# Two pairs of heads per run of scores, the first token's rows once for all batches, and another order of VectorE's steps, in a sink-window attention with Fourier mixing and a feed-forward block

## The chip, the core and the metric

The kernel runs on one core of a Trainium2 chip. The core has a matrix engine (TensorE; PE in the profile, with its weight loads as PEld), VectorE (DVE), ScalarE (ACT), GpSimd (POOL) and SyncE (SP), which issues most of the DMAs. Each engine works through its own list of instructions in order and waits on semaphores for the others. Sums of matmuls land in PSUM, which has eight banks; ACT and DVE copy them out. The metric is the device time of one execution in microseconds (us), the median of several runs. The profile is one execution; its span runs from its first to its last instruction.

## What is computed

Attention over 4 batches, 8 heads, 768 tokens of 64 values, in which each token sees the first four tokens (the sink) and the 127 before it and itself. Its output, 4 x 768 x 512, goes through a Fourier transform over tokens and channels, whose real part is added to it, and then through a feed-forward block.

```python
scores = scale * np.matmul(q, k.transpose(0, 1, 3, 2))
keep = is_sink | in_window
scores = np.where(keep, scores, -1000000000.0)
a = np.exp(scores - max); a = a / (sum(a) + 1e-09)
x = np.matmul(a, v)                       # then heads side by side: (4, 768, 512)
u = x + real(fft(fft(x, axis=1), axis=2))
un = (u - mean(u)) / sqrt(var(u) + 1e-06)
out = u + np.maximum(un @ w_ch1, 0.0) @ w_ch2
```

All of it is in 32-bit precision. Products that need more than one pass of the fast matmul type split a value into a high and a low part (names with `hi` and `lo`).

## The kernel before

**Steps.** The attention goes over 24 blocks g of 128 tokens (6 per batch), and in a block over 4 pairs of heads hp. One step s = 4 g + hp handles one pair; k = s % 4 is the place in the block. `window_attention` is a software pipeline: at step s, `scores` runs for step s itself, and the other stages run for earlier steps, by `STEP_LAG`: `merge` and `soft1` one step later, `expo` two, `trans_p` three (for two pairs at once, at even k), `copy_p` four, `newer_p` and `older_p` five, `av` seven (also at even k). Stages that run once a block have their distance in `BLOCK_AT`: `trans_sink` 7 (so at k = 3), `copy_sink` 8, `inverse` 7, `turn_x` 12, `store_x` 13, and `sink_lo`, once a batch, 2.

**What a step does.** `scores` (L721; L719 in the first block of a batch) multiplies 64-row halves of PE by the keys, for two heads side by side, into one of two PSUM buffers "s". On DVE, `merge` (L727) selects between two key blocks and `soft1` (L739) scales, masks and finds the maximum, which frees the buffer. ACT does the exponential (`expo`, L745). PE turns the result (`trans_p`, L770, bank "pt"), ACT copies it out (`copy_p`, L777), GpSimd cuts it into two triangles (L786, L794), and PE multiplies by the values (`av`, L808, output xt, on 64-column halves). `trans_sink` (L826) turns the sink's part, also in the bank "pt", and `copy_sink` (L831) copies it out. `turn_x` (L820, L822) and `store_x` (L836) bring the block into `u`.

**The order on each engine** up to step 97 (`CUT`) is written out by hand: `SCHEDULE[s >= 36][engine][k]` lists the stages, and between them the names in `EVENTS`: "A", "V", "G", "T" and the digits 0 to 3, places where work registered by `at(step, place, fn)` is put. "T" is work on PE, "V" and the digits are on DVE. "S" is work of SP's queue and runs ahead of the step's scores. From step 97 on a planner chooses the order, and it may set that work between the steps written by hand.

**The transform.** When the fourth block of a batch is stored (steps 25, 49, 73, 97), `fourier` registers its parts at distances from there. Folds (`fold_n`, `fold_m`, L348 to L358, on DVE and GpSimd) at 3, 4, 7, 8, 11 and 12, their split (L361 on ACT, `fold_lo`, L364, on DVE) three to four steps later; PE's first stage (`stage1`, L393) from 15 on; then its second (L420, L441). Each stage's result is copied out of the one bank "fft" (at k = 2 another bank, "x", is used in some steps), by `z_hi`, `z_lo`, `combine` and their like. For batches 0 to 2 many parts are cut in two, one in each of two steps.

**The first token.** Token 0 is no row of the six blocks of 128 that come out of attention; its output is made on 32 partitions (batch x head) at steps 10 to 20 and stored to DRAM (`x0_dram`). Each batch's `fourier` loads it broadcast to 33 partitions (`load_row`, L343), and at distance 5 copies its row into `u` (`put_row`, L379), at 8 folds it (`mid_sum`, L368), and at 10 splits it into rows 0 and 32 of `sph` (`mid_hi`, L371, and `mid_row`, L376), which PE's first stage reads.

**After attention** come the weight conversion (L600 to L602 on DVE), the first group of the feed-forward block (L638, L1139) and the five others (L638, L1313).

Of the kernel before, what the change touches and what calls it, by code (L numbers as in the profile page):

```python
# [11 lines left out]
F32 = mybir.dt.float32  # L12
# [7 lines left out]
P = 128  # L20
# [44 lines left out]
F_N, F_M, F_S, ROW = (3, 3), (4, 5), (6, 7), (5, 8, 10)  # L65
# [4 lines left out]

STEP_LAG = {"merge": 1, "soft1": 1, "expo": 2, "sink_p": 2, "trans_p": 3, "copy_p": 4, "newer_p": 5, "older_p": 5, "av": 7}
# [21 lines left out]
            ["merge", "inverse", "store_x", "sink_lo", "V", "soft1", 3, 0, 1, 2],  # L93
            [3, "merge", 1, "V", "soft1", "inverse", "store_x", 0, "sink_lo", 2],
            ["sink_lo", 0, "merge", 3, 1, "V", 2, "soft1", "store_x", "inverse"],
            ["merge", "inverse", 0, "soft1", "V", 3, "store_x", "sink_lo", 2, 1],
# [22 lines left out]
            ["merge", "inverse", "store_x", "sink_lo", "soft1", 3, 1, 0, "V", 2],  # L119
            [2, "merge", 0, "sink_lo", 3, 1, "V", "soft1", "inverse", "store_x"],  # L120
            ["sink_lo", 0, "merge", "soft1", 3, "V", 2, 1, "store_x", "inverse"],
            ["merge", 1, "inverse", 3, 2, "soft1", "store_x", "V", 0, "sink_lo"],
# [89 lines left out]
def kernel(  # L212
# [28 lines left out]
    x0_dram = dpool.tile([B * H, D], F32, name="x0d")  # L241

# [24 lines left out]
    def run(general):  # L267
        tag = "g" if general else ""
        with ExitStack() as p1:
# [58 lines left out]

            def fourier(b, at, ready):
# [11 lines left out]
                def load_row():  # L341
                    t_["x0"] = fw.tile([NR, DM], F32, tag="xr", name=f"xr_{b}")
                    nc.sync.dma_start(t_["x0"], x0_dram[H * b:H * b + H].rearrange("(o h) d -> o (h d)", o=1).broadcast_to([NR, DM]))  # L343
# [22 lines left out]
                def mid_sum():  # L366
                    r = t_["x0"]
                    V.tensor_tensor(r[:, 1:256], r[:, 1:256], r[:, 511:256:-1], op=ALU.add)  # L368

                def mid_hi():  # L370
                    (A.copy if b == B - 1 else V.tensor_copy)(sph[:NR, :257], t_["x0"][:, :257])  # L371

                def mid_row():
                    t = t_["x0"]
                    lo = sph[NR - 1:NR, :257]
                    V.tensor_tensor(lo, t[NR - 1:NR, :257], f32(lo), op=ALU.subtract)  # L376

                def put_row():
                    V.tensor_copy(u[NHALF][0:1], t_["x0"][0:1])  # L379
# [83 lines left out]
                at(1, "S", load_row)  # L463
# [10 lines left out]
                at(ready[0] + ROW[0], "V", put_row)  # L474
                at(ready[0] + ROW[1], "V", mid_sum)
                at(ready[0] + ROW[2], "A" if b == B - 1 else "V", mid_hi)
                at(ready[0] + ROW[2], "V", mid_row)
# [176 lines left out]
            def window_attention(fourier, load_constants):  # L654
                with ExitStack() as pa:
# [168 lines left out]
                    def trans_sink(g):  # L824
                        ps = ps_t.tile([P, P], F32R, tag="pt", name=f"pk_{g}")
                        T.transpose(ps, st.pop(("sk", g)).rearrange("p g h s -> p (g h s)"), ident_r)  # L826
                        st["pk", g] = ps
# [16 lines left out]
                    with ExitStack() as man:  # L844
# [117 lines left out]
                        for i in range(NS):  # L962
                            at(17 + i, "V", lambda i=i: first_row(i))

# [6 lines left out]
                        s = 0  # L971
                        extra.append(lambda name: ps_t.tile([P, 512], F32, tag="x", name=name)
                                     if s % NP in X_AT and not X_NOT[0] <= s <= X_NOT[1] and s < len(steps) - 2 else None)
                        while s < last:
# [19 lines left out]
                            if k == 3 and wraps:  # L994
                                load_qk(g + 2)
                            if s == 0:
# [3 lines left out]
                            for e in "AVGT":  # L1000
                                for op in SCHEDULE[s >= PHASE][e][k]:
                                    if op in EVENTS:
# [16 lines left out]
            def general_attention(fourier):  # L1019
                for b in range(B):  # L1020
# [74 lines left out]
                    ev = []  # L1095
# [506 lines left out]
```

## Time and profile before

| | |
|---|---|
| median of 3 runs | 768.49 us (767.43 to 771.24) |
| the profiled execution's own time | 768.74 us |
| its span | 767.0 us |
| mean granted clock of PE | 0.995 |
| score pairs in the trace | 96 steps: 320 matmuls L721, 64 matmuls L719 |
| softmax passes (L739) | 192, mean 285 ns |
| queue of SP | 94352 packets, 124.26 MB |

The views that follow in the prediction are read so. The page's first part gives each engine's busy time, its share of the span and its instructions. A view of stages gives the same for each stretch of time, with the granted clock as a share of full speed. A row of the view of waits says which instruction group waited for which, how long in all, how often, and the longest. The chain goes back from the last instruction to what released it at each step: a start, a length, and what ran. In a timeline, a start and a duration of each instruction; on DVE, the next starts before the last one's end is written, so the distance between starts is what one costs.

### The profile page before, as it was taken

How to read it: one execution, taken by the hardware profiler on the slowest of the kernel's cores; microseconds unless marked ns; L12 is line 12 of the kernel's file. 1: busy time of each engine (PE TensorE's matmuls, PEld its weight loads, DVE VectorE, ACT ScalarE, POOL GpSimd, SP SyncE). 2: the span in 40 equal slices, each digit the busy share in tenths (PEclk: the TensorE clock that was granted, in tenths of full speed). 3: DMA queues.
4: the chain of work that ended last, by engine and by line, in shares of the span. 5: the costliest groups of instructions: out<-in, count | busy, mean ns of one | idle time of the engine just before them, and what ended most of it. 6: DMA issues, size and time to landing. Idle time of an engine off the chain costs nothing.

```text
span 767.0 us, 14157 instructions
## 1 busy us (share of the span) xinstructions
PE 742.3 (97%) x4903; PEld 626.7 (82%) x4903; DVE 600.6 (78%) x1641; ACT 345.9 (45%) x896; POOL 181.6 (24%) x286
## 2 busy tenths in 40 slices
PE   7999998998999999999999999999999999999996
PEld 5666775766788778788989899899899998998995
DVE  6878588799799989969877978778895888764435
ACT  4877666666643223444545333333333333333330
POOL 2557267467574445400000000000000000000001
PEclk9999999999999999999999999999999999999998
DMA  9845514532313446323546757755577557556661
GB/s 294 277 112 165 144 56 151 160 104 94 111 56 138 138 165 219 110 110 141 190 151 247 227 160 231 230 171 191 170 226 235 173 172 243 160 176 188 208 193 60
DMA packets 95008, 129.40 MB, mean 169 GB/s; under 512 B 5932, under 2 KB 60844, under 8 KB 94544
## 3 DMA queue, kind: packets, MB, share of 16 engines
q1 hardware_dynamic: 94352, 124.26, 51.1%
q0 software_dynamic: 288, 3.76, 1.3%
q8 instruction: 41, 0.67, 0.4%
q10 hardware_dynamic: 288, 0.39, 0.1%
q14 instruction: 39, 0.32, 0.1%
HBM read 104.26 MB, written 24.13 MB: 167 GB/s over the span
## 4 chain that ended last, share of the span: by engine, by line
PE 78%; DVE 16%; issue 2%; ACT 1%; POOL 1%; DMA 1%; SPq 0%; DVEq 0%; ACTq 0%; POOLq 0%
PE h L638 31%; PE p L1313 25%; PE xt L808 5%; PE s L721 5%; PE o L1139 3%; PE pt L770 2%; PE za L393 2%; PE zb L393 1%; DVE f L348 1%; PE x L820 1%; DVE sm L739 1%; DVE gl L364 1%; PE zr L393 1%; DVE w2r L602 1%; DMA vt<-in_v_sink_dram 1%
## 5 line engine op out<-in xcount | busy, mean ns | idle before, releaser
L1313 PE MATMUL p<-w_ring,h_sums 128*128 128x256 f32 x936 | 131.3, 283 | 0.1
L1313 PEld LDWEIGHTS p<-w_ring,h_sums 128*128 128x128 f32 x936 | 122.9, 191 | 3.6 <-DVE u L1143 0.3
L1261 ACT CAST h_sums<-sums 128x256 fp32r<-128x256 f32 (+2 forms) x158 | 89.7, 568 | 70.5 <-PE p L1313 28.6
L1262 DVE TENSOR_TENSOR h_sums<-sums,h_sums 128x256 fp32r<-128x256 f32 (+2 forms) x158 | 98.3, 622 | 17.5 <-ACT h_sums L1261 16.5
L1313 PE MATMUL p<-w2t,h_sums 128*128 128x256 f32 x702 | 110.3, 283 | 0.0
L1335 POOL TENSOR_TENSOR u<-u,u 128x512 f32<-128x512 f32 x3 | 3.8, 1293 | 422.9 <-DVE u L1335 422.9
L1313 PEld LDWEIGHTS p<-w2t,h_sums 128*128 128x128 f32 x702 | 97.9, 191 | 3.1
L638 PE MATMUL h<-un_slots,w 128*128 128x512 f32 x396 | 96.5, 392 | 0.0
L638 PE MATMUL h<-un_last,w 128*128 128x512 f32 x396 | 96.4, 392 | 0.0
L638 PEld LDWEIGHTS h<-un_slots,w 128*128 128x128 f32 x396 | 72.7, 188 | 14.0
L638 PEld LDWEIGHTS h<-un_last,w 128*128 128x128 f32 x396 | 72.3, 188 | 14.4 <-DVE un_slots L553 0.7
L745 ACT ACTIVATE sm<-sm,mx 128x132 f32<-128x132 f32 x192 | 75.8, 399 | 14.4 <-DVE mx L739 14.4
L1475 ACT ACTIVATE sums<-h 128x512 f32<-128x512 f32 x40 | 23.9, 597 | 96.8 <-PE h L638 96.8
L721 PE MATMUL s<-ring,q 64*128 64x260 f32 x320 | 55.6, 430 | 7.2 <-DVE mx L739 7.2
L1163 DVE STREAM_TRANSPOSE unf<-un 32x128 f32<-32x128 f32 x192 | 58.1, 302 | 2.8
L1272 DVE TENSOR_TENSOR sums<-sums 128x256 f32<-128x256 f32 x39 | 16.4, 422 | 47.6 <-ACT sums L1475 47.3
L1443 ACT ACTIVATE sums<-h 128x512 f32<-128x512 f32 x40 | 23.9, 599 | 64.8 <-PE h L638 64.8
L739 DVE CUSTOM_DVE_ANT_0 sm<-s,mask 128x132 f32<-128x132 f32 x192 | 47.5, 285 | 4.5 <-PE s L719 2.4
L727 DVE COPY_PREDICATED s<-older,s 128x256 f32<-128x256 uint8 x80 | 33.8, 422 | 16.9 <-PE s L721 16.6
L721 PEld LDWEIGHTS s<-ring,q 64*128 64x128 f32 x320 | 25.0, 186 | 21.3 <-issue 10.0
L808 PE MATMUL xt<-ptl,ldv 128*64 128x128 f32 x384 | 39.8, 288 | 0.0
L745 ACT ACTIVATION_READ_ACCUMULATOR sm<-sm,mx 128x1 f32 x192 | 36.7, 191 | 0.0
(239 smaller groups left out, 1378.1 us busy)
## 6 DMA issues: line engine op xcount, KB each, us to landing
w_ring<-w2s SPq DMA_DIRECT2D x62, 512.0 KB, 4.3
w2t<-w2s SPq DMA_DIRECT2D x93, 256.0 KB, 3.2
raw<-in_moe_w_ch_dram SPq DMA_DIRECT2D x32, 512.0 KB, 3.3
w2s<-w_ring SPq DMA_DIRECT2D x16, 512.0 KB, 3.0
ldv<-in_v_dram SPq DMA_DIRECT2D x28, 256.0 KB, 2.8
ring<-in_qk_dram SPq DMA_DIRECT2D x24, 264.0 KB, 4.3
w2s<-w2t SPq DMA_DIRECT2D x24, 256.0 KB, 3.1
out_dram<-u SPq DMA_DIRECT2D x22, 256.0 KB, 4.6
```

The lines of the kernel that those rows point to most:

```text
L393: T.matmul(ps[:, :NK], a, c, start=i == 0, stop=i == len(mm) - 1)
L638: T.matmul(ps[:, :tb], a[:, cs], x[:, :, cc, :], start=n == 0, stop=n == 3 * NCC - 1)
L721: T.matmul(ps[:, j, :P + W], st["q", g][rows, hp, :], keys(g, 2 * hp + j), start=True, stop=True)
L727: V.copy_predicated(ps[:, :, P + NS:P + W], older[qi > 2], ps[:, :, 0:P])
L739: V.tensor_tensor_reduce(sm[:, h % 4], ps[:, j, P:P + W], mask[min(qi, 3)], -SCALE, 3.0e38, ALU.add, ALU.min, accum_out=mx[:, 0, h:h + 1])
L745: A.activation(sm[:, h % 4], sm[:, h % 4], AF.Exp, bias=mx[:, 0, h:h + 1], scale=-1.0, accum_out=mx[:, 1, h:h + 1])
L808: T.matmul(ps[D * j:D * j + D, p, :], st["v", kb(g) - i][:, h, :], a[:, h % 4, :], start=i == 0, stop=i == n - 1)
L1163: V.transpose(unf[32 * q:32 * q + 32, :, r], un[r].rearrange("p (c q j) -> p c q j", c=NCC, q=4)[:, :, q])
L1261: A.copy(hc_hi[:, left(a, n)], src)
L1262: V.tensor_tensor(hc_lo[:, left(a, n)], src, f32(hc_hi[:, left(a, n)]), op=ALU.subtract)
L1313: T.matmul(acc[i][:, 2 * P * tp:2 * P * tp + 2 * P], x, w, start=q == 0 and tp == 0 and n == 0, stop=q == end and n == 2, skip_group_check ...
L1443: A.activation(r4[:, 0].rearrange("p t w -> p (t w)"), ps, AF.Relu)
```

## The change

It has four parts.

1. Between steps 9 and 96, at odd k, PE's list no longer runs "T" and `trans_sink` at their place: they are put into `hold` and run in the next step, behind its scores. So scores of an odd step and of the even step after it stand next to each other. `bank` decides by the step to which the work belongs (`at_s`).
2. `trans_sink` uses the bank "fft" in place of "pt" as long as its step is under 36.
3. DVE's lists become the same in both phases: `merge` and `soft1` first in every step, then what belongs to that k, then the digit 1, then "V". (The digits 0, 2 and 3, which fall out, hold no work; stages appear only at the k at which they can run.)
4. The first token's rows are made once: `middle_rows` loads them for all four batches on four partitions at step 24, folds them at 26 (DVE), splits them at 27 (ACT) and 28 (DVE), and stores both parts to DRAM (`xm_dram`) at 29. Each batch then loads rows 0 and 32 of `sph` by DMA at distance 9, and `put_row` is a DMA at distance 5. `mid_sum`, `mid_hi` and `mid_row` are gone.

```diff
-F_N, F_M, F_S, ROW = (3, 3), (4, 5), (6, 7), (5, 8, 10)
+F_N, F_M, F_S, ROW = (3, 3), (4, 5), (6, 7), (9, 5)
+ROW_AT = 24, 26, 27, 28, 29
+HOLD = 9, 97
...
         "V": [
-            ["merge", "inverse", "store_x", "sink_lo", "V", "soft1", 3, 0, 1, 2],
-            [3, "merge", 1, "V", "soft1", "inverse", "store_x", 0, "sink_lo", 2],
-            ["sink_lo", 0, "merge", 3, 1, "V", 2, "soft1", "store_x", "inverse"],
-            ["merge", "inverse", 0, "soft1", "V", 3, "store_x", "sink_lo", 2, 1],
+["merge", "soft1", 1, "V"],
+            ["merge", "soft1", 1, "V", "store_x"],
+            ["merge", "soft1", "sink_lo", 1, "V"],
+            ["merge", "soft1", "inverse", 1, "V"],
         ],
...
-            ["merge", "inverse", "store_x", "sink_lo", "soft1", 3, 1, 0, "V", 2],
-            [2, "merge", 0, "sink_lo", 3, 1, "V", "soft1", "inverse", "store_x"],
-            ["sink_lo", 0, "merge", "soft1", 3, "V", 2, 1, "store_x", "inverse"],
-            ["merge", 1, "inverse", 3, 2, "soft1", "store_x", "V", 0, "sink_lo"],
+["merge", "soft1", 1, "V"],
+            ["merge", "soft1", 1, "V", "store_x"],
+            ["merge", "soft1", "sink_lo", 1, "V"],
+            ["merge", "soft1", "inverse", 1, "V"],
...
+            def middle_rows(b, n, at):
+                x = fw.tile([B, DM], F32, tag="xr", name=f"xr_{b}")
+                xm = fw.tile([B, 2, DM // 2 + 1], F32R, tag="xm", name=f"xm_{b}")
+                def load():
+                    nc.sync.dma_start(x[:n], x0_dram[H * b:H * (b + n)].rearrange("(o h) d -> o (h d)", o=n))
+                def fold():
+                    V.tensor_tensor(x[:n, 1:256], x[:n, 1:256], x[:n, 511:256:-1], op=ALU.add)
+                def hi():
+                    A.copy(xm[:n, 0], x[:n, :257])
+                def lo():
+                    V.tensor_tensor(xm[:n, 1], x[:n, :257], f32(xm[:n, 0]), op=ALU.subtract)
+                def store():
+                    nc.sync.dma_start(xm_dram[b:b + n], f32(xm[:n]))
+                for s, e, fn in zip(ROW_AT, "SVAVS", (load, fold, hi, lo, store)):
+                    at(s, e, fn)
...
                 def load_row():
-                    t_["x0"] = fw.tile([NR, DM], F32, tag="xr", name=f"xr_{b}")
-                    nc.sync.dma_start(t_["x0"], x0_dram[H * b:H * b + H].rearrange("(o h) d -> o (h d)", o=1).broadcast_to([NR, DM]))
+                    nc.sync.dma_start(f32(sph[:NR:NR - 1, :257]), xm_dram[b])
...
                 def put_row():
-                    V.tensor_copy(u[NHALF][0:1], t_["x0"][0:1])
+                    nc.sync.dma_start(u[NHALF][0:1], x0_dram[H * b:H * b + H].rearrange("(o h) d -> o (h d)", o=1))
...
-                at(1, "S", load_row)
+                at(ROW[0], "S", load_row)
...
-                at(ready[0] + ROW[0], "V", put_row)
-                at(ready[0] + ROW[1], "V", mid_sum)
-                at(ready[0] + ROW[2], "A" if b == B - 1 else "V", mid_hi)
-                at(ready[0] + ROW[2], "V", mid_row)
+                at(ready[0] + ROW[1], "S", put_row)
...
                     def trans_sink(g):
-                        ps = ps_t.tile([P, P], F32R, tag="pt", name=f"pk_{g}")
+                        pool, tag = (ps_fft, "fft") if NP * g + BLOCK_AT["trans_sink"] < PHASE else (ps_t, "pt")
+                        ps = pool.tile([P, P], F32R, tag=tag, name=f"pk_{g}")
...
+                        middle_rows(0, B, at)
...
+                        def run_held(step):
+                            nonlocal at_s
+                            at_s = step
+                            run_ev(step, "T")
...
                             lag(scores, s, 0)
                             if k == 3 and wraps:
                                 load_qk(g + 2)
+                            held, hold = hold, []
+                            for fn in held:
+                                fn()
+                            at_s = s
...
                                 for op in SCHEDULE[s >= PHASE][e][k]:
-                                    if op in EVENTS:
+                                    if e == "T" and k % 2 and HOLD[0] <= s < HOLD[1]:
+                                        if op == "T":
+                                            hold.append(lambda s=s: run_held(s))
+                                        elif op == "trans_sink" and k == BLOCK_AT[op] % NP:
+                                            hold.append(lambda g=(s - BLOCK_AT[op]) // NP: 0 <= g < NQ and trans_sink(g))
+                                    elif op in EVENTS:
```

More of the change, by code (lines that the diff above doesn't have):

```diff
@@ L241 @@
     x0_dram = dpool.tile([B * H, D], F32, name="x0d")
+    xm_dram = dpool.tile([B, 2, DM // 2 + 1], F32, name="xmd")
     prm = cpool.tile([P, 2, 2], I32, name="prm")
@@ L364, in fold_lo @@
                     V.tensor_tensor(gl[:, j], t_.pop(("g", j)), f32(gh[:, j]), op=ALU.subtract)
[L366 to L376, printed above, removed]
                 def put_row():
-                    V.tensor_copy(u[NHALF][0:1], t_["x0"][0:1])
+                    nc.sync.dma_start(u[NHALF][0:1], x0_dram[H * b:H * b + H].rearrange("(o h) d -> o (h d)", o=1))
                 def stage1(kind, mc, part, parts):
@@ L970, in window_attention @@
                         }
-                        s = 0
+                        s = at_s = 0
                         extra.append(lambda name: ps_t.tile([P, 512], F32, tag="x", name=name)
-                                     if s % NP in X_AT and not X_NOT[0] <= s <= X_NOT[1] and s < len(steps) - 2 else None)
+                                     if at_s % NP in X_AT and not X_NOT[0] <= at_s <= X_NOT[1] and at_s < len(steps) - 2 else None)
+                        hold = []
+                        def run_held(step):
+                            nonlocal at_s
+                            at_s = step
+                            run_ev(step, "T")
                         while s < last:
@@ L1095, in general_attention @@
                     ev = []
+                    middle_rows(b, 1, lambda s, e, fn: fn())
                     fourier(b, lambda d, e, f: ev.append((d, ENGINES.index(e), len(ev), f)), FOLD_AT)
```

## The prediction

> **What bounds the kernel now.** The page's busy shares come first.
>
> ```profile
> PE 742.3 (97%) x4903; PEld 626.7 (82%) x4903; DVE 600.6 (78%) x1641; ACT 345.9 (45%) x896; POOL 181.6 (24%) x286
> ```
>
> That is a mean over two halves. The change touches the attention steps, up to 208 us, so next comes the view of busy times by stage (busy us of each engine, granted clock, DMA share).
>
> ```profile
> 20.00:55.00 35.00, 33.84 (x332) 24.00 (x330) 27.47 (x136) 27.28 (x110) 20.34 (x44) 1.00 0.64 200
> 55.00:71.00 16.00, 13.56 (x115) 8.64 (x117) 14.66 (x62) 12.55 (x49) 11.54 (x20) 1.00 0.47 127
> 71.00:104.00 33.00, 33.00 (x279) 25.37 (x279) 19.31 (x84) 20.57 (x75) 14.22 (x28) 1.00 0.44 128
> 104.00:134.00 30.00, 27.29 (x216) 19.43 (x216) 25.37 (x91) 19.13 (x74) 22.29 (x38) 0.94 0.40 120
> 164.00:186.00 22.00, 18.78 (x154) 13.59 (x155) 19.62 (x68) 13.11 (x47) 15.95 (x27) 1.00 0.37 112
> 186.00:208.00 22.00, 21.87 (x176) 16.20 (x173) 17.05 (x68) 13.80 (x49) 12.47 (x23) 1.00 0.36 121
> 208.00:280.00 72.00, 69.32 (x401) 58.29 (x401) 70.58 (x130) 26.21 (x59) 37.59 (x35) 1.00 0.33 112
> ```
>
> PE has no idle time at 71 to 104 and loses 2.44, 2.71 and 3.22 us in the three stages at 55, 104 and 164 us, where the folds of batches 0, 1 and 2 lie and DVE is 85 to 92% busy. From 208 to 280 us DVE is full (70.58 of 72) and bounds. Third view: who PE waited for, 20 to 225 us (us, times, longest).
>
> ```profile
> PE s L721 <- DVE mx L739: 5.1, 5, 2.4
> PE pk L826 <- ACT pta L777: 2.4, 7, 0.6
> PE x L820 <- DVE un_slots L553: 1.0, 1, 1.0
> ```
>
> So scores wait for soft1 of two steps earlier (their PSUM buffer), and trans_sink waits for copy_p (it shares the bank "pt"). The last view is the chain that ended last: start, us, what.
>
> ```profile
> 25.91 1.08 PE s L721 x8
> ...
> 45.91 0.65 PE s L719 x8
> ...
> 74.67 0.64 PE s L721 x4
> 75.31 1.08 PE za L393 x5
> ...
> 77.03 1.02 PE xt L808 x16
> ...
> 96.58 0.43 PE s L719 x4
> ```
>
> A pair of heads alone between other work takes 0.64 us; two pairs in a row take 1.08, not 1.28. In a batch's first block it is 0.43 alone and 0.65 for two. So leaving and re-entering a run of scores costs 0.20 us.
>
> **Part 1: two pairs per run.** The hold takes T events and trans_sink out from between the scores of odd step s and even step s+1, for s = 9 to 95. Scores alone stand in the other odd steps already (the x8 rows). Counting: trans_sink lies in every step with s%4 = 3 from 11 to 95, 22 pairs; T events at s%4 = 1 are the transform's parts in steps 41, 45, 49, 53, 57 (batch 0), 65, 69, 73, 77, 81, 85 (batch 1), 89, 93 (batch 2), 13 pairs. 35 x 0.20 = **7.0 us**. Nothing shows what av (xt) costs behind a held full-array part instead of behind scores. From above: as behind scores, 1.02, no change. From below: the chain has half an av (x8) at 0.61, so eight more matmuls cost 0.41 and entry about 0.20; were entry free, 35 x 0.20 = 7 more.
>
> ```profile
> 61.18 0.61 PE xt L808 x8
> ```
>
> I take 1.02, the row of the same 16 matmuls, and allow 2 us of the rest in the range. The Trainium skill, "TensorEngine Tiling (Array Packing)", Key Properties, says that changing the tiling mode drains TensorE; av splits the columns, so by it the entry stays paid and the sum is the same 7.0; no run here shows it yet.
>
> The held part waits for nothing new: its inputs are a step old. Its result comes later against its consumers: z_hi/z_lo and combine of the even step now follow scores of that step. The next part in the same bank is behind av alone or av and pt, 1.0 to 1.6 us, and no longer behind a 0.64 pair too, while an evacuation takes about 0.6 on ACT (the row of a wider copy, in part 2). I cost it at 0; uncovered, it would be up to 0.6 at some ten parts, 6 us.
>
> **Part 2: trans_sink.** Its wait is for a copy on ACT:
>
> ```profile
> 42.23 0.59 ACT pta L777
> ...
> 42.95 0.25 PE pk L826
> ```
>
> It now follows both pairs, 0.44 us later than before, and up to step 35 has the "fft" bank, idle then, so copy_p of the same step no longer holds it. The pk row says 2.4 us in seven waits, none over 0.6. Only those behind step 35 depend on the 0.44. I take all, **2.4**; half of it if ACT is later than that.
>
> **Part 3: VectorE's order.** Here is DVE before the longest wait, that of step 62's scores.
>
> ```profile
> 120.20 1.36 DVE L364 TENSOR_TENSOR gl<-f,gh 128x512 fp32r<-128x512 f32 x1
> 121.49 1.11 DVE L348 TENSOR_TENSOR f<-us,us 128x512 f32<-128x512 f32 x1
> 122.53 0.42 DVE L727 COPY_PREDICATED s<-older,s 128x256 f32<-128x256 uint8 x1
> 122.86 0.52 DVE L358 TENSOR_TENSOR f<-f 128x255 f32<-128x255 f32 x1
> 123.30 0.28 DVE L739 CUSTOM_DVE_ANT_0 sm<-s,mask 128x132 f32<-128x132 f32 x1
> ```
>
> Between merge (L727) and soft1 (L739) lies fold_m, 0.52. The new list puts it behind soft1; gl and the next fold stay ahead, as they belong to the step before. The price of that wait goes on after it.
>
> ```profile
> 123.95 1.24 PE s L721 x4
> 125.19 1.90 PE xt L808 x16
> ```
>
> Against 0.64 and 1.02 that is 1.5 us more; the granted clock of this stage is 0.94, of the others 1.00. So DVE's waits cost 5.1 + 1.0 + 1.5 = 7.6 us.
>
> **Part 4: the first token's rows.** Per batch four instructions leave DVE (min/median/max ns):
>
> ```profile
> L368 DVE TENSOR_TENSOR xr<-xr x4: 404/436/1486, 58.4 to 219.2; 33x255 f32<-33x255 f32 x4
> L376 DVE TENSOR_TENSOR sph<-xr,sph x4: 418/735/777, 63.1 to 225.6; 1x257 fp32r<-1x257 f32 x4
> L371 DVE CAST sph<-xr x3: 282/757/1408, 62.8 to 176.5; 33x257 fp32r<-33x257 f32 x3
> L379 DVE COPY u<-xr x2: 407/408/410, 53.2 to 163.1; 1x512 f32<-1x512 f32 x2
> L379 DVE COPY us<-xr x2: 846/868/889, 105.5 to 218.1; 1x512 f32<-1x512 f32 x2
> ```
>
> From the timeline they sum to 2.6 us in batch 0, 2.8 in batch 1 and 3.0 in batch 2. Two on four partitions come back, once, at about 0.4 each (the L368 minimum): DVE's steps at 20 to 55 us have 7.5 us idle for them. Where they leave the stages at 104 and 164 us, DVE falls from 25.37 to 22.6 and from 19.62 to 16.6, beside PE work of about 27.29 - 1.5 - 1.2 = 24.6 and 18.78 - 0.8 = 18.0 us (six and four pairs at 0.2). That is enough in the sum, not in each burst: gl, fold, and merge and soft1 of two steps (0.34 + 2 x 0.21 each by their starts) are 1.36 + 1.11 + 2 x 0.77 = 4.0 us. Between two runs without a transform part PE has these, with pk 0.25 and xt 1.02:
>
> ```profile
> 24.65 0.59 PE pt L770 x4
> 25.24 0.44 PE x L820 x4
> ```
>
> That is 2.3 us and, with the run's own 1.08, 3.4, so some 0.6 us of wait can be left in such a step. POOL (22.29 of 30) fills up too. Of the 7.6 I take three quarters, **5.7**; the ends are 2 (bursts stay) and 7.6.
>
> In the last batch, in DVE's own stage, these pieces of the chain go:
>
> ```profile
> 218.14 0.77 DVE us L379
> ...
> 219.17 0.40 DVE xr L368
> ...
> 225.64 0.78 DVE sph L376
> ```
>
> That is 1.95, and **1.9** taken. ACT's copy there goes too, off the path.
>
> SP gets, once, a load, a store that waits for DVE, and per batch a load and a copy into u that waits for both first folds. Behind the waiting ones stand the loads of later keys and values.
>
> ```profile
> SPq L690 <- PE xt L808: 59.6, 12, 8.7
> ldv<-in_v_dram SPq DMA_DIRECT2D x28, 256.0 KB, 2.8
> ```
>
> SP already sits 59.6 us waiting for buffers; a load lands in 2.8 us and its values are due five steps (some 11 us) later, so a wait of 2 or 3 us is covered; without cover it is as long as the fold is late, about 2 us, at each of four batches. In the last batch the weight loads stand behind it. I take 0, with 8 as the other end.
>
> **Part 5: the start.** At step 4 soft1 passes the other masks.
>
> ```profile
> PE s L721 <- DVE mx L739: 2.0, 2, 1.6
> ```
>
> Within 4 to 50 us this is that wait mainly (1.6), but the masks then delay the next soft1. I take **0.5** of 0 to 1.6.
>
> **The sum.** 7.0 + 2.4 + 5.7 + 1.9 + 0.5 = 17.5. The profiled execution took 768.74 (span 767.0 and 1.7 around it), 0.25 above the median: 768.74 - 17.5 = 751.2. Behind 280 us nothing is touched and the rest moves up whole.
>
> **Rivals.**
> - DVE and POOL at their ceiling. The fold waits return before the second pair of a run. For: 4.0 against 3.4 above, and POOL at 74% of that stage. Against: both fit in the sum. It keeps 7.0, 1.9, half of part 2 and 0.5, 10.6 in all: 758. Chance 0.20.
> - The gain stays in attention. DVE's full stage from 208 us would not start earlier. For: 70.58 of 72. Against: its work is released by the steps before it, and DVE has 5 us idle at 186 to 208. Then 1.9 remains, or little more: 766. Chance 0.06.
> - Slower by the clock. PE waits in one piece at the second pair. If DVE needs 1.4 us more per burst than the rows say, each of nine fold steps waits the 2.4 us that was followed by slow matmuls: 9 x (2.4 + 1.5) = 35 instead of 7.6, less 11.8 for the other parts: 784. Against: DVE loses 2.6 us or more per batch. Chance 0.06. The Trainium skill, "TensorE: Matmul & The Clock Gate", Part 1, puts the drop behind an idle window of about 3.4 us; the trace shows 2.4 us of recorded idle enough once. By the page's figure the waits alone would count, 22 instead of 7.6, and the time would be 771.
>
> **How the numbers follow.** The forecast, 745 to 756, has 0.68. Its low end is 768.7 less 7.0 + 2, 2.4, 7.6, 1.9 and 1.6, which is 746, and 1 for folds that DVE and POOL slow less. The range that holds 8 in 10 reaches through the first rival and over part of the open ends of parts 1 and 4 (6 and 8 us more): 743 to 762. About 0.5% (3.8 us) is what a measurement tells from no change: faster by more 0.88, within 0.06, slower 0.06.
>
> **What would show it.** Nearly every run of scores from step 9 on is x8 at 1.08 in the chain; PE's wait for ACT at pk is gone; the stage with the batch-1 folds has clock 1.00 and PE idle under 1 us; L368, L371, L376 and L379 are gone from DVE. Wrong would be: xt dearer than 1.02 behind a held part, PE idle before the second pair in the fold steps, or SP waits for folds with DVE idle behind a late weight load after 208 us.

## The result and the profile after

| | before | after |
|---|---|---|
| median of 5 runs | 768.49 us (767.43 to 771.24) | 761.03 us (760.66 to 762.94) |
| the profiled execution's own time | 768.74 us | 761.03 us |
| its span | 767.0 us | 759.3 us |

The ratio is 0.9903, with a 95% interval of 0.9884 to 0.9922: 7.5 us faster, where 17.3 was forecast. The direction was right and the time lies in the range; the size was less than half. Of the executions behind the medians of this document, one of e15, of 2483 us, is left out.

In the changed kernel the lines have new numbers: scores L731 (L729 in a batch's first block), merge L737, soft1 L749, av L818, the folds L373 and L383, gl L389, stage1 L406, trans_sink L837.

The page of the changed kernel, the row of busy times:

```profile
PE 736.3 (97%) x4903; PEld 627.3 (83%) x4903; DVE 597.6 (79%) x1628; ACT 345.0 (45%) x896; POOL 179.7 (24%) x286
```

PE has 6.0 us less to do, DVE 3.0 us and 13 instructions less. The view of busy times by stage comes next, with the stages of the folds of batches 1 and 2 and DVE's own stage; the columns are those of the same view before.

```profile
104.00:128.00 24.00, 22.18 (x185) 15.93 (x185) 21.14 (x77) 16.52 (x60) 19.36 (x32) 1.00 0.48 144
159.00:178.00 19.00, 17.17 (x148) 12.81 (x146) 17.61 (x62) 12.42 (x45) 15.28 (x25) 1.00 0.42 126
201.00:272.00 71.00, 68.25 (x400) 58.12 (x399) 68.91 (x126) 25.35 (x57) 37.37 (x35) 1.00 0.34 113
```

The clock of the batch-1 stage is 1.00, as forecast. But PE still idles for 1.8 us in each of the two fold stages. The view of PE's waits, 20 to 225 us, says for what:

```profile
PE s L731 <- DVE mx L749: 3.7, 5, 0.9
PE s L731 <- PE s L731: 1.3, 4, 0.6
PE xt L818 <- POOL pta L804: 0.9, 1, 0.9
```

Scores still wait for soft1: 3.7 us where it was 5.1. The second row, 1.3 us, are second pairs of a run, whose wait the view puts down to the first pair. PE's wait for ACT at pk, 2.4 us before, is no longer in the list.

**Where the time went.** In the timeline of PE, the steps can be cut at the first scores matmul, and each piece of a step (scores, av, a transform's part) costs from its start to the next start. The sum of the least costs that such a piece has, over the runs of this study and with the same neighbours, is here called PE's own work, and the rest is waiting. That divides steps 8 to 94 as follows (us; worked out from the timelines, as are the other tables below):

| | before | after |
|---|---|---|
| step 8 starts at | 17.7 | 17.6 |
| PE's own work, steps 8 to 94 | 174.8 | 168.2 |
| waiting in these steps | 14.8 | 14.2 |
| step 95 (the last scores) starts at | 207.28 | 199.91 |
| from there to the end of the span | 559.75 | 559.40 |

So PE's own work fell by 6.6 us, close to the 7.0 of the forecast, and the waiting, which should have fallen by 8.1, fell by 0.6. The order of DVE, the bank and the rows removed much more waiting than that, as the next section shows; the pairs brought it back.

Rows of the timeline of PE after show the pairs at work (start, length, what):

```profile
194.82 1.15 PE L731 MATMUL s<-ring,q 64*128 64x260 f32 x8
195.90 0.44 PE L406 MATMUL zr<-cst,gl 128*128 128x386 f32 x1
...
196.98 0.44 PE L818 MATMUL xt<-ptl,ldv 128*64 128x128 f32 x4
...
198.00 0.66 PE L554 MATMUL unx<-ident,un 128*128 128x128 f32 x4
```

From start to start the run of two pairs takes 1.08, and av behind the held part 1.02, as behind scores. This is the value that the prediction had to choose between bounds. The Trainium skill, "TensorEngine Tiling (Array Packing)", Key Properties, says that a change of the tiling mode drains TensorE; the 1.02 that stays agrees with it.

And this is what brings the waiting back, at step 61 in the batch-1 stage. First three rows of the timeline of DVE, then one of POOL's, then two of PE's:

```profile
116.19 0.69 DVE L389 TENSOR_TENSOR gl<-f,gh 128x512 fp32r<-128x512 f32 x1
116.79 1.76 DVE L373 TENSOR_TENSOR f<-us,us 128x512 f32<-128x512 f32 x1
118.48 0.42 DVE L737 COPY_PREDICATED s<-older,s 128x256 f32<-128x256 uint8 x1
```

```profile
116.28 1.73 POOL L373 TENSOR_TENSOR f<-us,us 128x512 f32<-128x512 f32 x1
```

```profile
118.01 0.71 PE L731 MATMUL s<-ring,q 64*128 64x260 f32 x4
119.60 0.71 PE L731 MATMUL s<-ring,q 64*128 64x260 f32 x4 [0.88 <-DVE mx L749]
```

DVE begins merge (L737) for the step before at 118.48, behind gl and the fold. The row of the first pair ends 0.71 behind 118.01; the second pair waits 0.88 us more for the soft1 behind that merge, and the run is broken.

### The profile page after: what moved, and what is told of

Same layout as the page of the kernel before. It is cut to its first block, busy times and chain, and to the rows that moved or that the text cites. A ratio compares the mean times of both kernels' runs of the same rounds, so it can differ in the third digit from the quotient of the medians.

```text
span 759.3 us, 14166 instructions
## 1 busy us (share of the span) xinstructions
PE 736.3 (97%) x4903; PEld 627.3 (83%) x4903; DVE 597.6 (79%) x1628; ACT 345.0 (45%) x896; POOL 179.7 (24%) x286
## 4 chain that ended last, share of the span: by engine, by line
## 5 line engine op out<-in xcount | busy, mean ns | idle before, releaser
L1291 DVE TENSOR_TENSOR h_sums<-sums,h_sums 128x256 fp32r<-128x256 f32 (+2 forms) x158 | 98.3, 622 | 17.3 <-ACT h_sums L1290 16.3
L731 PE MATMUL s<-ring,q 64*128 64x260 f32 x320 | 50.4, 415 | 7.1 <-DVE mx L749 5.0
L749 DVE CUSTOM_DVE_ANT_0 sm<-s,mask 128x132 f32<-128x132 f32 x192 | 48.9, 292 | 8.1 <-PE s L729 2.2
L731 PEld LDWEIGHTS s<-ring,q 64*128 64x128 f32 x320 | 26.2, 185 | 21.5 <-issue 7.4
L818 PE MATMUL xt<-ptl,ldv 128*64 128x128 f32 x384 | 39.3, 285 | 0.0
L737 DVE COPY_PREDICATED s<-older,s 128x256 f32<-128x256 uint8 x80 | 33.5, 419 | 7.0 <-PE s L731 6.9
```

The costliest lines, as they stand in the source:

```text
L731: T.matmul(ps[:, j, :P + W], st["q", g][rows, hp, :], keys(g, 2 * hp + j), start=True, stop=True)
L737: V.copy_predicated(ps[:, :, P + NS:P + W], older[qi > 2], ps[:, :, 0:P])
L749: V.tensor_tensor_reduce(sm[:, h % 4], ps[:, j, P:P + W], mask[min(qi, 3)], -SCALE, 3.0e38, ALU.add, ALU.min, accum_out=mx[:, 0, h:h + 1])
L818: T.matmul(ps[D * j:D * j + D, p, :], st["v", kb(g) - i][:, h, :], a[:, h % 4, :], start=i == 0, stop=i == n - 1)
L1291: V.tensor_tensor(hc_lo[:, left(a, n)], src, f32(hc_hi[:, left(a, n)]), op=ALU.subtract)
```

## The experiments

The times of whole executions differ by 1 or 2 us for reasons away from the change (the last section), and those of one kernel by 4 us and more (e2: 762.0 to 766.2). So besides the ratio each run is read by the start of step 95 in its profile ("S95"), where attention ends on PE. S95 holds the start too, which differs between profiles (step 8 starts at 17.2 to 18.3 us in the kernels with the masks at steps 4 and 6); the column "11 to 95" is the time from the start of step 11 to that of step 95, 185.42 us before and 178.25 after. These columns come from one execution of each kernel. Each group has its own runs of the kernel before; its median was 768.4 for e1 to e4, 768.6 for e5 to e8, 768.2 for e9 to e12, 767.3 for e13 to e15 and 768.9 for e16 and e17.

| run | us | ratio (95% interval) | S95 | 11 to 95 | waiting, steps 8 to 94 |
|---|---|---|---|---|---|
| e1 hold alone | 768.67 | 1.0008 (0.9993 to 1.0022) | 207.99 | 186.68 | 22.6 |
| e2 without the hold | 764.37 | 0.9943 (0.9926 to 0.996) | 200.66 | 179.00 | 8.3 |
| e3 old order of DVE | 762.91 | 0.9921 (0.9896 to 0.9946) | 203.18 | 179.11 | 16.6 |
| e4 old rows | 766.63 | 0.9978 (0.9965 to 0.9991) | 205.50 | 180.90 | 19.2 |
| e5 gl on ACT, its remainder left out | 760.43 | 0.9891 (0.9869 to 0.9913) | 196.34 | 174.22 | 10.1 |
| e6 = e5 without the hold | 760.58 | 0.9909 (0.9882 to 0.9937) | 198.88 | 177.00 | 6.3 |
| e7 masks earlier | 760.79 | 0.9893 (0.9872 to 0.9915) | 198.70 | 178.07 | 14.0 |
| e8 V ahead of 1 | 761.99 | 0.9907 (0.9885 to 0.9928) | 199.46 | 177.44 | 13.3 |
| e9 gl later | 762.92 | 0.9929 (0.9913 to 0.9945) | 201.08 | 178.96 | 14.9 |
| e10 = e9 without the hold | 764.49 | 0.9953 (0.9935 to 0.9971) | 201.00 | 179.69 | 9.0 |
| e12 = e9 and e8 | 762.47 | 0.9931 (0.9914 to 0.9947) | 199.81 | 177.94 | 13.9 |
| e11 = e12, e7, rows on POOL | 760.39 | 0.9901 (0.9883 to 0.9919) | 198.20 | 177.98 | 13.9 |
| e13 = e7 and e8 | 758.18 | 0.9883 (0.9856 to 0.991) | 196.95 | 177.22 | 13.1 |
| e14 = e13 and e5 | 754.13 | 0.9825 (0.9799 to 0.9851) | 192.79 | 173.04 | 9.0 |
| e15 = e14 without the hold | 758.32 | 0.9873 (0.9847 to 0.9899) | 196.57 | 176.62 | 5.9 |
| e16 = e13, odd folds later | 757.09 | 0.985 (0.9834 to 0.9867) | 195.99 | 176.15 | 12.1 |
| e17 = e16 without the hold | 758.18 | 0.9864 (0.9848 to 0.9881) | 197.17 | 177.37 | 6.7 |

**One part alone, or one part undone.** e1 is the kernel before with the hold and nothing else of the change.

```diff
+HOLD = 9, 97
...
+                                    if e == "T" and k % 2 and HOLD[0] <= s < HOLD[1]:
+                                        if op == "T":
+                                            hold.append(lambda s=s: run_held(s))
...
```

> The kernel before with the hold alone (old VectorE lists, old rows, trans_sink in its old bank). Theory A (the pairs give the whole gain, and the waits that the other three parts take away come back at other places): 761 to 763, PE work of steps 8 to 94 about 7 us less than before, its waits about as before. Theory B (order, bank and rows each hold a share of the gain): 764 to 766.

It gained nothing: 1.0008, above the ranges of both theories. PE's own work is 6.6 us shorter here too, and the waits are 7.8 us longer. The view of PE's waits, 20 to 225 us, and that of the two fold stages:

```profile
PE s L722 <- DVE mx L740: 9.7, 8, 2.8
```

```profile
104.00:128.00 24.00, 20.12 (x164) 14.48 (x163) 19.66 (x74) 14.72 (x52) 19.50 (x32) 0.93 0.37 104
162.00:190.00 28.00, 23.23 (x176) 17.23 (x173) 21.46 (x74) 15.31 (x54) 18.50 (x30) 0.88 0.36 107
```

The wait for soft1 went from 5.1 to 9.7 us and its longest from 2.4 to 2.8, and the granted clock fell to 0.93 and 0.88 behind it. With the old order and the rows on DVE, the pairs' saving is eaten whole. The theory that the pairs give the gain alone falls.

e2 is the changed kernel without the hold.

```diff
-HOLD = 9, 97
+HOLD = 97, 97
```

> The changed kernel without the hold: scores alone in their steps as before, with the new VectorE lists, the rows made once and the early trans_sink in the other bank. Theory A: 767 to 769, as before. Theory B: 763 to 765, because waits of 3 to 5 us go even without pairs.

Its 764.37 lies in theory B's range. It keeps 4.0 us of the gain by the medians, and 6.6 of the 7.4 us by S95. Its waiting is 8.3 us where the kernel before has 14.8, so order, bank and rows removed 6.5 us of waits without the pairs; forecast were 8.1. With the pairs on top, S95 moves by 0.75 us more. The medians of the two are 3.3 us apart; 1.9 us of that is the end, which is the longer one of two in e2's profile (561.28 us behind step 95, against 559.40), and the rest isn't explained. The wait for soft1 has fallen to 0.2 us, the last row of its view of PE's waits, 20 to 225 us:

```profile
PE xt L818 <- POOL pta L804: 1.2, 2, 0.9
PE pk L837 <- ACT pta L787: 0.8, 2, 0.6
...
PE s L731 <- DVE mx L749: 0.2, 1, 0.2
```

e3 has the old lists of DVE, e4 the old rows (four row instructions per batch on DVE, `load_row` broadcast, no `middle_rows`).

```diff
-["merge", "soft1", 1, "V"],
+            ["merge", "inverse", "store_x", "sink_lo", "V", "soft1", 3, 0, 1, 2],
...
```

> The changed kernel with the old VectorE lists. Theory A: 760 to 762, no different from the changed kernel. Theory B (soft1 first is needed where two scores stand in a row): 764 to 767, with longer waits of scores for soft1 in the fold steps.

```diff
-                at(ready[0] + ROW[1], "S", put_row)
+                at(ready[0] + ROW[0], "V", put_row)
+                at(ready[0] + ROW[1], "V", mid_sum)
...
-                        middle_rows(0, B, at)
```

> The changed kernel with the first token's rows made for each batch as before. Theory A: 760 to 763. Theory B: 764 to 766, since 2.6 to 3.0 us per batch are back on DVE in the stages where it is full.

e3's time, 762.91, lies between the two ranges, e4's, 766.63, above both. Their S95 misleads: in both profiles scores wait over 2 us near the start (2.55 at 13.7 us and 2.34 at 15.3), and the granted clock falls to 0.50 behind that, so step 11 starts 2.4 and 2.9 us later than in the changed kernel, ahead of most of what the two edits touch. The views of stages of e3 and of e4 (the clock is the third number from the end):

```profile
18.00:22.00 4.00, 4.00 (x21) 2.53 (x21) 1.90 (x10) 2.46 (x12) 1.51 (x5) 0.50 1.03 424
```

```profile
18.00:22.00 4.00, 3.87 (x20) 2.48 (x22) 2.15 (x13) 2.43 (x11) 1.52 (x5) 0.50 1.02 425
```

Undone one at a time, and read from step 11 on, the hold costs 0.75 us, the order 0.9 and the rows 2.7. That makes 4.3, less than the 7.2 of the whole change, while the hold alone gives -1.3. By the medians, which hold the end and the clock of each execution too, it is 3.3, 1.9 and 5.6, more than the 7.5 of the whole. So what each of order and rows is worth alone is not settled. In neither reading are the parts a sum: each is worth what the others leave of DVE's waits.

**Is it DVE?** e5 puts gl of batches 0 to 2 on ACT as a plain copy, so that gl holds the folded value and the remainder is left out; e6 is the same without the hold.

```diff
-                    V.tensor_tensor(gl[:, j], t_.pop(("g", j)), f32(gh[:, j]), op=ALU.subtract)
+                    if tail:
+                        V.tensor_tensor(gl[:, j], t_.pop(("g", j)), f32(gh[:, j]), op=ALU.subtract)
+                    else:
+                        A.copy(gl[:, j], t_.pop(("g", j)))
```

> The changed kernel, with the nine fold_lo of batches 0 to 2 on ACT, as plain copies, so gl holds the folded value itself and not what is left of it, and DVE has about 7 us less in the fold steps. Theory B (the pairs save PE 6.5 us, but scores then wait for DVE's bursts in the fold steps): 756 to 758, and the waits of steps 33 to 36, 57 to 66 and 81 to 86 fall from 6.3 to 3 us or less. Theory C (the waits come from the held parts' late results and from GpSimd, not from the length of DVE's bursts): 760 to 762.

> The same without the hold. Theory B: 762 to 764, hardly faster than the changed kernel without the hold (764.4), because without pairs PE is slower than DVE in most of these steps; so the hold is worth 5 to 6 us here and 3.4 there. Theory C: the hold is worth the same 3 to 4 us in both.

With the lighter DVE the pairs are worth 2.8 us from step 11 on (174.22 against 177.00), not 0.75: more than in the changed kernel, as theory B says, but half of its 5 to 6. The waits of the steps that e5's expectation names fall by 3.9 of 6.3 us, as B has it. The times do not show it: e5's 760.43 lies in the range of theory C, and e6's 760.58 is no different. One reason is the end, the longer one in e5's profile (561.0 us behind step 95) and the shorter in e6's (559.5); the last section comes back to that. So B rests here on the traces alone, and it stays open whether the time of gl itself matters or its meetings with GpSimd, which leave DVE with it.

**Two waits outside the folds.** e7 passes the masks at steps 1 and 4 and not 4 and 6; e8 puts "V" ahead of 1 in the third list of each phase.

```diff
-                        at(4, "V", other_masks)
-                        at(6, "V", last_mask)
+                        at(1, "V", other_masks)
+                        at(4, "V", last_mask)
```

> The changed kernel with the masks of later blocks made at step 1, where DVE waits for scores, and the last mask at step 4. If the waits of steps 5 and 7 (1.3 and 0.7 us) are DVE's masks alone: 758.5 to 760, step 8 at about 15.6 us and not at 17.6. If data of block 2 is what comes late there: 760.5 to 762.

```diff
-            ["merge", "soft1", "sink_lo", 1, "V"],
+            ["merge", "soft1", "sink_lo", "V", 1],
```

> The changed kernel with the place V ahead of the digit 1 in steps with k = 2. If the 1.0 us wait behind step 71 comes from DVE standing idle for a held part's result with statistics queued behind it: 759.5 to 760.5 and that wait gone. If other places pay for it (copies out of PSUM later): 761 to 762.

In e7 step 8 starts at 16.5 and not 17.6 (15.6 was expected), and S95 moves by 1.2, nearly all of it at the start. In e8 a wait of 0.97 us at step 71 is gone, and the time from step 11 to step 95 is 0.8 us less. That wait was the price of a held part: its result zr is copied out late, and DVE sits idle for it with the statistics of the next block queued behind. The timeline of DVE of the changed kernel:

```profile
140.06 0.55 DVE L418 TENSOR_TENSOR zr<-zr,zr 1x386 fp32r<-1x386 f32 x1 [1.03 <-ACT zr L411]
140.65 1.29 DVE L524 BATCH_NORM_STATS2 bn<-u 128x6 f32<-128x512 f32 x2
```

By the medians neither can be told from the changed kernel; both times lie in the range of the rival in their expectation, and both profiles have the longer end.

**Bunching or load?** In e9 gl of the first two block pairs is issued a step later, so that DVE has the same instructions but no step with both gl and a fold. e10 is e9 without the hold.

```diff
-                    at(k + F_S[1], "V", lambda j=j: fold_lo(j))
+                    at(k + F_S[1] + (not tail and j < 2), "V", lambda j=j: fold_lo(j))
```

> The changed kernel with one edit: the low half of a fold (gl) of the first two block pairs of batches 0 to 2 is issued one step later, so that it no longer lies in one step with the next pair's first fold. VectorE has the same instructions, only spread. Theory B as it stands (the pairs' saving on PE comes back as waits for VectorE's bursts): the fold steps' waits of PE, 5.5 us in the changed kernel, halve; the last scores of attention (step 95) start at 197 to 198 us and not at 199.9; the kernel takes 758 to 759.5 us. Rival D (it is VectorE's sum of work in those stages, not its bunching): step 95 stays at 199.5 to 200.5 and the time at 760 to 762. Rival E (later gl makes the transform's parts late, which then wait themselves): step 95 at 200.5 or later, PE's waits for gl appear.

> As e9, and without the hold (the scores of neighbouring steps in pairs are taken apart again). B: once the bursts are spread the pairs are worth more than the 0.75 us of the changed kernel against e2, 2 to 4 us of the 6.5 that PE's own work is shorter: step 95 at 200 to 201, the kernel 2 to 3 us behind e9. D: the hold is worth 0.75 us again. In either case the sum of least durations of PE's pieces over steps 8 to 94 is 174.7 us here and 168.3 in e9.

My theory of bunching fell: the waits moved and did not shrink (steps 57 to 66 take 21.7 us where they took 21.8, steps 27 to 36 18.4 against 17.2). At S95 the hold looks worth nothing here (201.08 against 201.00), but e9 starts step 8 0.8 us later; from step 11 on the hold is worth 0.73 us, as in the changed kernel, which is rival D. e9's S95 and time lie in the range of rival E, but its sign, waits of PE for gl, is not in the view of PE's waits. This speaks for DVE's load over these steps, not for the one step with both. e12 adds e8's edit to e9, e11 adds e7's and puts the two additions of `middle_rows` on GpSimd.

```diff
-                for s, e, fn in zip(ROW_AT, "SVAVS", (load, fold, hi, lo, store)):
+                for s, e, fn in zip(ROW_AT, "SGAGS", (load, fold, hi, lo, store)):
```

> As e9, and in every third step of four the transform's parts of VectorE stand ahead of the second softmax list entry 1, as in e8, where this took away the wait of 0.97 us at step 71. If the two waits are separate, step 95 starts 0.4 to 1.0 us ahead of e9's and the time is 757 to 759.

> All of e9 and e12, the masks of e7 at steps 1 and 4, and the two additions of the first token's rows on GpSimd instead of VectorE (0.73 us and a low half behind it at steps 26 to 28, where PE waited 0.8 us at step 27). If the waits are separate ones, step 95 starts at 195.5 to 197 us and the kernel takes 756 to 758. If each wait taken away is found again at the next step (GpSimd has 19.36 of 24 us in the stage of the batch-1 folds), step 95 is within 0.5 us of e12's.

e12 lost the wait at step 71 again and nothing else, and missed its 757 to 759 by the time (762.47, with the longer end). e11 missed its 195.5 to 197: S95 moved by 1.6 us, as much as step 8 starts earlier, and for the rows on GpSimd a wait of 0.6 us at step 27 went and one of 0.95 came at step 30.

**Do the causes add up?** e13 is the changed kernel with e7's and e8's edits, e14 also has e5's, e15 is e14 without the hold.

> The changed kernel with the edits of e7 and e8 together: the masks at steps 1 and 4, and the transform's part of VectorE ahead of entry 1 in every third step of four. Nothing is left out. If the wait at step 71 (0.97 us) and the start (1.2 us in e7) are separate from the fold steps, the last scores of attention (step 95) start at 197.5 to 198.3 us instead of 199.9, and the kernel takes 758.5 to 760.5 us, by which way the end goes (559.4 or 561.0 us behind step 95, and 1.7 around the span).

> As e13, and the low halves of the folds of batches 0 to 2 are plain copies on ScalarE instead of subtractions on VectorE, as in e5 (the remainder is left out, so this shows what a lighter VectorE gives, not a kernel to use). If the pairs' saving was eaten by VectorE's load in the fold steps and by the two places above, and these add up, step 95 starts at 194.0 to 194.6 us (196.3 in e5, less 1.0 and 1.2) and the kernel takes 755 to 757.5 us. If a wait taken away comes back at the next step, step 95 stays above 195.

> As e14 without the hold. The pairs were worth 0.75 us at step 95 in the changed kernel (199.9 against 200.7 in e2) and 2.5 us with the lighter VectorE (196.3 against 198.9). If VectorE's load and the held parts' late results are what takes back the 6.5 us, they are worth 3 to 4 us here: step 95 at 197.3 to 198.3 us. If the pairs are worth no more than 2.5 us whatever else waits, step 95 is at 196.5 to 197.

They do: the pairs are worth 3.6 us from step 11 on in this surrounding (173.04 against 176.62) and 4.2 by the medians (754.13 against 758.32). e13, e14 and e15 came out 0.5 to 1.2 us below the S95 that the first case of their expectations has (e15's lies in the range of its rival for that reason), mostly because step 8 starts at 15.6 to 15.8 us in them, some 0.8 earlier than in e7. The view of e14's two fold stages and its waits of PE, 20 to 225 us, against those of the changed kernel above:

```profile
102.00:126.00 24.00, 22.79 (x196) 16.79 (x197) 19.27 (x79) 18.09 (x65) 19.73 (x34) 1.00 0.54 166
154.00:172.00 18.00, 18.00 (x157) 13.87 (x157) 16.21 (x62) 14.24 (x49) 15.72 (x27) 1.00 0.44 133
```

```profile
PE za L409 <- ACT asb L445: 1.2, 1, 1.2
PE pt L783 <- ACT skt L845: 1.2, 3, 0.8
PE xt L821 <- POOL pta L807: 0.7, 1, 0.7
PE s L734 <- PE s L734: 0.7, 3, 0.3
...
PE s L734 <- DVE mx L752: 0.6, 1, 0.6
```

The wait for soft1 fell from 3.7 to 0.6 us and PE idles no more in batch 2's stage. What is left in attention are copies of ACT and triangles of GpSimd that PE meets sooner (the first row lies at 218 us, behind step 95). By stage (us; PE's own work is 2.2 us less with the hold in the fold stages, 4.3 in the others):

| steps | before | e2 no hold | after | e15 no hold | e14 |
|---|---|---|---|---|---|
| 27 to 36 (folds of batch 0) | 18.5 | 17.0 | 17.2 | 16.5 | 16.8 |
| 57 to 66 (batch 1) | 24.0 | 20.7 | 21.8 | 20.7 | 20.6 |
| 81 to 87 (batch 2) | 17.4 | 15.5 | 15.5 | 14.1 | 13.5 |
| the others of 8 to 94 | 129.7 | 129.9 | 127.9 | 129.4 | 126.4 |

From e2 to the changed kernel the pairs cost 1.3 us in the fold stages, where they shorten PE's work by 2.2, and gain 2.1 of the 4.3 in the others. From e15 to e14 they gain 0.6 and 3.0.

**Two engines at the same time.** In step 61 above, the two halves of a fold run at the same time, on DVE for 1.76 us and on POOL for 1.73. In e16 POOL's half is issued a step later; e17 is e16 without the hold.

```diff
-                    at(k + F_N[1], e1, lambda j=j: fold_n(eng[e1], j, 1))
+                    at(k + F_N[1] + (not tail), e1, lambda j=j: fold_n(eng[e1], j, 1))
```

> As e13, and the odd half of each fold (the f on GpSimd) of batches 0 to 2 is issued one step later than the even half on VectorE; both were issued in the same step. In the changed kernel the f on VectorE takes 0.68 us with GpSimd quiet and up to 1.76 us (1.73 on GpSimd) where the two run at once; PE's longest wait in the batch-1 stage, 0.88 us at step 61, lies behind such an f. If their meeting is what makes VectorE late in the fold steps, the f's on VectorE come down towards 0.7 us, the stages of batches 1 and 2 (steps 57 to 66 and 81 to 87, 21.78 and 15.47 us in e13) get shorter by 1 to 2 us together, step 95 starts at 195 to 196 us and the kernel takes 756 to 757.5. If GpSimd only meets another instruction of VectorE then, the stages stay within 0.5 us and the time at 757.5 to 759.

> As e16 without the hold. The pairs are worth about 1.7 us at step 95 with VectorE's full load (0.75 in the changed kernel and 1.0 for the wait at step 71 that e8 took away) and 3.8 us with the low halves off VectorE (e14 against e15). If the meeting of the folds on VectorE and GpSimd is the load that matters, e17's step 95 is 2.5 us or more behind e16's; if it is VectorE's number of instructions, 1.5 to 2 us.

e16 is the fastest kernel here that leaves nothing out: 757.09, a ratio of 0.985 (0.9834 to 0.9867), whose interval lies apart from that of the changed kernel (0.9884 to 0.9922), though not from e13's. But the reason I gave is only in part the one at work. Steps 57 to 66 stay at 21.9 us (21.8 in e13) and steps 81 to 87 lose 0.4 of 15.5; steps 27 to 56 gain 0.7. The timelines of DVE and of POOL in e16 say why:

```profile
105.41 1.69 DVE L389 TENSOR_TENSOR gl<-f,gh 128x512 fp32r<-128x512 f32 x1
107.03 0.68 DVE L373 TENSOR_TENSOR f<-us,us 128x512 f32<-128x512 f32 x1
```

```profile
105.27 1.29 POOL L373 TENSOR_TENSOR f<-us,us 128x512 f32<-128x512 f32 x1
```

This fold on DVE is down to 0.68, and gl, beside POOL's half now, is at 1.69. GpSimd meets another instruction instead: over the nine folds of this row the median falls only from 1.10 to 1.02 us. The pairs are worth 1.2 us here (195.99 against 197.17), below both bounds of the expectation.

## Why the prediction was right and wrong

**The step that failed is the sum**: 7.0 for the pairs and 5.7 for DVE's waits, counted side by side, with the line "both fit in the sum" against the rival in which the waits return. Each term was near what it is by itself: the pairs took 6.6 us out of PE's own work, and order, bank and rows without the pairs took 6.5 us of waits away (e2), where 2.4 + 5.7 = 8.1 stood. Together they gave 7.2 us in steps 8 to 94. When PE is quicker by 6.6 us, DVE has that much less time for the same work, and it was 85 to 92% busy in the fold stages. Of the 5.9 us by which the pairs lengthen the waiting (8.3 in e2, 14.2 after), 3.5 lie in the fold stages and 1.6 at two steps behind a held part (part 1 below). The comparison of busy sums (22.6 us of DVE beside 24.6 of PE) showed only that both fit when nothing ever waits; the burst that the prediction worked out beside it, 4.0 against 3.4 us, was charged at a quarter of the 7.6 and its waits came in each of batches 0 to 2. Its size was not the fault: gl and the fold take 2.29 us from start to start at step 61, where 1.36 + 1.11 stood. But such folds became more common: the median of the nine folds of this row is 1.10 us after, where it had been 0.78. The groups by line, before and after (min/median/max ns):

```profile
L348 DVE TENSOR_TENSOR f<-us,us x9: 672/783/1291, 99.5 to 228.0; 128x512 f32<-128x512 f32 x9
```

```profile
L373 DVE TENSOR_TENSOR f<-us,us x9: 676/1097/1765, 96.6 to 221.6; 128x512 f32<-128x512 f32 x9
```

Point by point:

- **Part 1.** Entry cost, count and av behind a held part (1.02) were right; 6.6 and not 7.0. That a held part's later result costs nothing was wrong: 0.97 us at step 71 (e8 took it away), and 0.65 at step 92, not tested by itself, where the first part of zr waits for DVE's step on za (L421), the result of a held part. That wait's row in the view of PE's waits:

```profile
PE zr L406 <- DVE za L421: 0.4, 1, 0.4
```

- **Part 2.** The wait at pk went, as said.
- **Part 3.** Clock 1.00, right. The waits for soft1 fell by 1.4 us instead of 5.1 less a quarter, with the pairs in place.
- **Part 4.** The rows had their share: with the old ones the steps from 11 on take 2.7 us more (e4). SP's wait for the fold came, longer than thought, and no loss behind it shows, as taken: counted from step 95, one weight load is issued 1.9 us later than before, the others at the same time or up to 3.0 us earlier. The view of SP's waits, 190 to 260 us:

```profile
SPq L392 <- DVE f L373: 5.2, 1, 5.2
```

- **The last batch.** 1.95 us of row instructions left DVE's own stage, and the way from step 95 to the end shrank by 0.35, not 1.9. In the 72 us behind step 95 DVE is busy 69.15 us where it was 69.90: part of the 1.95 went to longer instructions (what stretches them is shown below), and in the rest DVE idles. What holds the end there instead is open; whether the late weight load has a part in it was not tried.
- **Part 5.** Step 8 starts 0.16 us earlier, not 0.5: the masks' wait moved to steps 5 and 7. At steps 1 and 4 step 8 starts 1.0 (e7) and 1.9 us (e13) earlier, though kernels with the masks at steps 4 and 6 also range from 17.2 to 18.3, so that the 0.16 can't be told from none.

**The rivals.** The first, in which the fold waits return before the second pair of a run, is what happened, with the rows of step 61 as its picture. Its price was off: it let the pairs keep 7.0 and stood at 758. The gain that stays in attention did not occur, since step 95's 7.4 us came through to the end. Nor did the clock fall; e1 shows that this rival was real for the pairs without the other parts, with 0.93 and 0.88.

What stays open: of the 6.6 us, 3.6 are recovered in e14. The remaining 3.0 lie, by its views, in waits for ACT and GpSimd and at broken runs, and no run took those away.

## What to carry to other kernels

A saving on the bounding engine is worth at a given place no more than the slack of the engine that feeds it there; work out that engine's time per period against the shortened period before adding the saving to a removed wait, as both may be the same microseconds. Test a part by taking it alone and by leaving it out: the hold is worth -1.3 us in the kernel before, 0.75 in the changed one and 3.6 with a lighter DVE. Where DVE and GpSimd worked at the same time here, an instruction's duration depended on what the other was doing (a fold on DVE took 0.68 to 1.77 us), so a row's mean can't be carried to a new order. And before two profiles are compared by one point in time, look whether they start alike.

## What the runs showed of the hardware

**DVE and GpSimd take turns.** Some 25 us behind step 95, the same instructions in the same order on DVE go one of two ways in the 16 profiles with the new rows (before, e1 and e4 have another order there). The changed kernel, timeline of POOL and then of DVE:

```profile
224.90 1.90 POOL L637 TENSOR_TENSOR w<-cv,w 128x512 fp32r<-128x512 f32 x1 [3.80 <-issue]
```

```profile
224.98 0.68 DVE L611 SCALAR_TENSOR_TENSOR w2r<-raw,w2r 128x512 int32<-128x512 int32 x1
...
229.26 1.31 DVE L611 SCALAR_TENSOR_TENSOR cv<-raw,cv 128x512 int32<-128x512 int32 x1
```

and the same instructions in e8:

```profile
224.49 1.29 POOL L637 TENSOR_TENSOR w<-cv,w 128x512 fp32r<-128x512 f32 x1 [3.80 <-issue]
```

```profile
224.56 1.77 DVE L611 SCALAR_TENSOR_TENSOR w2r<-raw,w2r 128x512 int32<-128x512 int32 x1
...
229.12 1.51 DVE L610 TENSOR_SCALAR w2r<-raw 128x512 int32<-128x512 int32 x1
```

Either DVE goes first (0.68) and POOL takes 1.90, or POOL goes first (1.29) and DVE takes 1.77: 1.29 beside 0.6 of waiting, or 0.68 beside 1.1. At 229 us a second meeting costs e8's DVE 1.10 (1.51 against the 0.41 of that row in the changed kernel) and the changed kernel's 0.63 (1.31 against 0.68). In all 1.09 + 1.10 - 0.63 = 1.56 us. The time from step 95 to the end is 559.2 to 559.9 us in 12 of the 19 profiled executions of this study and 561.0 to 561.3 in the other seven. Of the 16 profiles, nine go the first way (POOL 1.90 to 1.92 us) and all are of the shorter kind; seven go the second (DVE 1.75 to 1.77) and all are of the longer. So these rows account for the 1.6 us between kernels that differ only in attention. What decides who is first was not settled. The Trainium skill, "SBUF — State Buffer", in the section on its two separate sides, says that the port pair which the two engines share is a lock held for a whole instruction, so that the second blocks fully; these rows agree, down to the fold of step 61: POOL's 1.73 ends at 118.01, and DVE's 1.76, begun at 116.79, ends 0.54 behind that.

**The clock falls behind some single waits.** In the changed kernel PE has no wait over 1.3 us from 4 to 225 us, and its granted clock there is 1.00. In the kernel before it is 0.50 from 124 to 127 us, behind the wait of 2.4 us, and in e1 it falls to 0.50 or 0.51 behind waits of 2.8, 2.2 and 1.4 us. But the length of the wait alone does not decide: behind 2.2 us in e5 and 2.0 in e8, at 15 us, the clock stays at 1.00, and behind 1.3 us in e4, at 63 us, it is 0.57 over the four microseconds from 64. What else decides is open. And between executions of one kernel the mean granted clock differs: in the runs of the kernel before beside e13, those at 0.997 took 766.7 to 767.6 us and those at 0.990 to 0.992 took 769.6 to 771.6.
